# Another order for the first 45 microseconds of a fused attention-plus-MLP block: x on two load queues, the first weights' low parts on GpSimd, x's last 64 columns transposed once

## The chip, the cores and the metric

The kernel runs on one core of one Trainium2 chip. The metric is the device time of one execution in microseconds (us). Before the change the median of three runs is 1194.38 us, from 1193.45 to 1194.89.

## The reference, cut to what matters

The input x has 2048 rows of 576 columns. The output is the sum of x itself, a sliding dilated attention on the layer-normalised x, and a two-layer MLP with ReLU on the same normalised x.

```python
x = A_x                                   # 1 x 2048 x 576
xn = _layernorm(x, axis=-1)
# attention: 32 heads of 18, each row sees 8 rows: itself and 2, 4, ... 14 rows back
qkv = xn @ wqkv                           # 576 x 1728
attn = softmax(q . k[pos - 2*w] * 18**-0.5)   # w = 0..7, rows before 0 masked
a = (sum over w of attn * v[pos - 2*w]) @ wo  # 576 x 576
# MLP
b = relu(xn @ w1) @ w2                    # 576 x 4608, 4608 x 576
return x + a + b
```

## The kernel before, in words

The rows are cut into two phases of 1024 rows, and each phase into eight tiles of 128 rows, named x0 to x7 here. For every tile, `stats` computes mean and variance on VectorE (DVE) and the inverse root on GpSimd (POOL), `norm` applies them on VectorE or, with `act=True`, on ScalarE (ACT), and `make_xt` transposes the result on TensorE (PE) into PSUM and from there writes a high part (ScalarE, rounded to the fast matmul format) and a low part (VectorE, the difference). All matrices are held as such a pair. A product is three sums of terms: high by high, low by high and high by low; the list `TERMS` gives fourteen matmuls for 576 columns, of which the first four use the high part of x and of the weight, the next four the low part of x, the ninth the mixed block of the last 64 columns, and the last five the low part of the weight.

The 576 columns are four blocks of 128 and a rest of 64 (`DR`). In the rest block, high and low part of x share one 128-row tile (`mix`): rows 0 to 63 high, 64 to 127 low. Before the change the 64 columns are first written twice side by side (line 261 for x, line 411 for the attention's output), so that one transpose of 128 columns puts them on both halves of the partitions.

The MLP is a row of slots. Slot n belongs to a phase, a chunk of three hidden blocks of 128, a pair of tiles (`tb`) and one hidden block. `h_mm(n)` multiplies w1 by the pair's transposed x (fourteen matmuls of 256 columns) and evicts the ReLU as a high part on ScalarE (line 447) and a low part on VectorE (line 448). `o_mm(n)` multiplies that by w2 (twelve matmuls of 288 columns) into the PSUM tiles `po`; after the third block of a chunk the sums are added to x on VectorE (line 471). The loop at the end of `tile_body` issues h_mm two slots ahead of o_mm. h0 to h2 read the transposed x0 and x1, h3 to h5 read x2 and x3, h6 to h8 read x4 and x5, h9 to h11 read x6 and x7.

Weights come through a ring of four staging tiles `st` (loads on SP's queue), and `two` splits each into high (line 146, ScalarE) and low (line 143, VectorE). The step at which a split is issued is set by the plan; for the first chunk the six steps stand in `HEADW` (three for w1, three for w2). The next load of the ring is issued when a split has read its staging tile.

The order in the opening is written by hand. Before the loop the loads, the statistics and the norms of x0 to x2, the splits of the first two w1 blocks (`held` puts their low parts behind the low parts of x) and the transposes of x0 and x1 are issued. The list `HEAD` places the remaining `stats`, `norm` and `xt` calls at a step; 0 puts the call behind h_mm of that step, 1 behind o_mm; the last field says whether `norm` runs on ScalarE, or whether `xt` uses the big PSUM tiles `po`. Every engine works its instructions off in the order of issue. Attention work starts later and is spread over VectorE by estimated times (`run_bg`).

## Time and profile before

| | |
|---|---|
| median of three runs | 1194.38 us (1193.45 to 1194.89) |
| profiled execution | 1194.74 us, of which the span is 1193.0 us |
| TensorE (PE) busy | 1183.8 us, 99% of the span |
| VectorE (DVE) busy | 812.5 us, 68% |
| ScalarE (ACT) busy | 310.5 us, 26% |
| GpSimd (POOL) busy | 40.1 us, 3% |
| mean granted TensorE clock | 0.998 |

The profile gives per engine the time in which an instruction ran. A view of waits names who waited for whom. A timeline gives start and duration in us, engine, source line, operation, the tile written and the tiles read, shape and count, and in brackets the idle time before and who ended it. The chain of waits follows the work back from the last instruction. PE's busy time is a modelled one, since matmuls are pipelined; the distance from start to start is what counts.

### The profile page before, as it was taken

To read this page: it belongs to the slowest core of one execution; us is meant where nothing else is said; L and a number is where in the kernel's file an instruction comes from. 1 tells how busy PE (TensorE), PEld (TensorE's weight loads), DVE (VectorE), ACT (ScalarE), POOL (GpSimd) and SP (SyncE) were. 2 spreads that over 40 slices of the span, in tenths; PEclk is the share of its full clock that TensorE was granted. 3 is DMA by queue.
4 is the path that set the end of the run, shared out by engine and by line. 5 is a ranking of instruction groups with operands and counts; after the bars stand their busy time and mean duration, and the time that the engine had idled before them with its cause. 6 is when DMAs were issued, how large, how long until landed. Compare 5 with 4: busy or idle time off the path is not lost.

```text
span 1193.0 us, 21739 instructions
## 1 busy us (share of the span) xinstructions
PE 1183.8 (99%) x9016; PEld 1172.8 (98%) x9016; DVE 812.5 (68%) x1269; ACT 310.5 (26%) x790; POOL 40.1 (3%) x63
## 2 busy tenths in 40 slices
PE   8999999999999999999999999999999999999998
PEld 7999999999999999999999999999999999999998
DVE  7516875888687578875573278858767875886732
ACT  5422222131222222322233123122221322222210
POOL 2000000010000000000120000000100000000000
PEclk9999999999999999999999999999999999999999
DMA  5312122130321311402242113031302312212002
GB/s 172 84 32 82 42 76 55 38 107 1 98 58 44 86 33 43 114 11 73 91 130 74 46 54 90 22 85 29 86 21 79 83 38 79 63 42 73 21 1 80
DMA packets 84883, 75.67 MB, mean 63 GB/s; under 512 B 6592, under 2 KB 68288, under 8 KB 84784
## 3 DMA queue, kind: packets, MB, share of 16 engines
q1 hardware_dynamic: 82256, 66.08, 19.7%
q10 hardware_dynamic: 2528, 8.20, 2.4%
q8 instruction: 71, 1.16, 0.4%
q14 instruction: 28, 0.23, 0.1%
HBM read 61.34 MB, written 4.72 MB: 55 GB/s over the span
## 4 chain that ended last, share of the span: by engine, by line
PE 98%; DVE 1%; SPq 0%; ACT 0%; DMA 0%; issue 0%; DVEq 0%; ACTq 0%
PE ph L112 39%; PE po L112 38%; PE pm L112 20%; PE pm L273 1%; PE pm L274 0%; DMA st<-in_w 0%; SPq L235 0%; DVE pr L380 0%; DVE pr L373 0%; SPq L157 0%; SPq L162 0%; SPq L161 0%; PE po L273 0%; ACT xn L257 0%; ACT xn L256 0%
## 5 line engine op out<-in xcount | busy, mean ns | idle before, releaser
L112 PE MATMUL ph<-xT,w1t 128*128 128x256 f32 x4032 | 514.2, 279 | 1.3 <-ACT xT L276 0.6
L112 PEld LDWEIGHTS ph<-xT,w1t 128*128 128x128 f32 x4032 | 491.6, 188 | 2.0 <-ACT xT L276 0.8
L112 PE MATMUL po<-w2t,hhi 128*128 128x288 f32 x2304 | 400.5, 296 | 0.4 <-DVE w2t L143 0.3
L112 PEld LDWEIGHTS po<-w2t,hhi 128*128 128x128 f32 x2304 | 337.0, 188 | 2.0 <-DVE w2t L143 0.5
L447 ACT ACTIVATE hhi<-ph 128x256 fp32r<-128x256 f32 x288 | 110.2, 382 | 531.8 <-PE ph L112 512.5
L112 PE MATMUL po<-w2t,hlo 128*128 128x288 f32 x1152 | 244.7, 293 | 0.0
L448 DVE SCALAR_TENSOR_TENSOR hlo<-ph,hhi 128x256 fp32r<-128x256 f32 x288 | 121.7, 423 | 169.1 <-ACT hhi L447 167.8
L471 DVE TENSOR_TENSOR x<-po,x 128x576 f32<-128x576 f32 x192 | 143.9, 757 | 69.8 <-PE po L112 66.3
L112 PE MATMUL pm<-wq,xT 128*128 128x432 f32 x896 | 185.5, 358 | 0.0
L112 PEld LDWEIGHTS po<-w2t,hlo 128*128 128x128 f32 x1152 | 183.7, 188 | 0.0
L112 PEld LDWEIGHTS pm<-wq,xT 128*128 128x128 f32 x896 | 163.8, 188 | 5.6
L343 DVE TENSOR_TENSOR pr<-qo,k 128x1152 f32<-128x1152 f32 x64 | 85.9, 1349 | 0.0
L373 DVE TENSOR_TENSOR pr<-lg,v 128x1152 f32<-128x1152 f32 x64 | 85.0, 1352 | 0.3
L346 DVE TENSOR_REDUCE lg<-pr 128x64 f32<-128x1152 f32 x64 | 85.0, 1343 | 0.0
L143 DVE TENSOR_TENSOR w2t<-st,w2t 128x576 fp32r<-128x576 f32 x72 | 54.3, 755 | 45.0 <-ACT w2t L146 44.7
L380 DVE TENSOR_TENSOR pr<-pr 128x288 f32<-128x288 f32 (+1 forms) x128 | 70.5, 602 | 0.1
L143 DVE TENSOR_TENSOR w1t<-st,w1t 128x640 fp32r<-128x640 f32 x72 | 59.0, 820 | 15.0 <-ACT w1t L146 14.8
L146 ACT ACTIVATE w2t<-st 128x576 fp32r<-128x576 f32 x72 | 49.1, 684 | 45.0 <-PE po L112 31.0
L146 ACT ACTIVATE w1t<-st 128x640 fp32r<-128x640 f32 x72 | 53.0, 737 | 13.2 <-DMA st<-in_w 13.2
L312 ACT ACTIVATE k<-pm 128x144 f32<-128x144 f32 x64 | 18.7, 292 | 142.8 <-PE pm L112 142.6
L112 PE MATMUL pm<-wq,oT 128*128 128x288 f32 x352 | 51.7, 299 | 0.0
L112 PEld LDWEIGHTS pm<-wq,oT 128*128 128x128 f32 x352 | 47.9, 188 | 1.7
(63 smaller groups left out, 398.0 us busy)
## 6 DMA issues: line engine op xcount, KB each, us to landing
st<-in_w SPq DMA_DIRECT2D x72, 288.0 KB, 3.0
st<-in_w SPq DMA_DIRECT2D x72, 256.0 KB, 3.0
st<-in_wqkv SPq DMA_DIRECT2D x32, 216.0 KB, 3.0
st<-in_w SPq DMA_DIRECT2D x144, 32.0 KB, 2.7
out<-x SPq DMA_DIRECT2D x16, 288.0 KB, 2.1
x<-in_x SPq DMA_DIRECT2D x15, 288.0 KB, 3.9
k<-k ACTq DMA_DIRECT2D x8, 441.0 KB, 3.9
v<-v ACTq DMA_DIRECT2D x8, 441.0 KB, 4.6
```

The lines of the kernel that those rows point to most:

```text
L112: nc.tensor.matmul(o, l, r, start=start, stop=stop)
L143: nc.vector.tensor_tensor(lo, src, f32(hi), op=ALU.subtract)
L146: nc.scalar.activation(hi, src, AF.Copy)
L273: nc.tensor.transpose(pa[:, k, :], src[:, k * P : (k + 1) * P], ident)
L312: nc.scalar.activation(k[:, W - 1 + i, :], pq[:, 1, :], AF.Copy)
L343: nc.vector.tensor_tensor(pr[i], q, window(k, i), op=ALU.mult)
L346: nc.vector.tensor_reduce(lg[:, i], pr.pop(i).rearrange(heads, d=Dh), axis=AX.X, op=ALU.add)
L373: nc.vector.tensor_tensor(pr[i].rearrange(heads, d=Dh), e, window(v, i).rearrange(heads, d=Dh), op=ALU.mult)
L380: nc.vector.tensor_tensor(o, z[:, 0:n], z[:, n : 2 * n], op=ALU.add)
L447: nc.scalar.activation(hi, pt, AF.Relu)
L448: nc.vector.scalar_tensor_tensor(lo, pt, 0.0, f32(hi), op0=ALU.max, op1=ALU.subtract)
L471: nc.vector.tensor_tensor(acc, PO[k][:, :, 0:D2], acc, op=ALU.add)
```

## The change

- The loads of x1, x2 and x3 are issued on ScalarE's queue; x0 (in two halves) and x4 to x7 stay on SP's. All four staging tiles are loaded before x4. The `Exp` that loads ScalarE's table now follows ScalarE's three loads.
- While `early` holds (the six splits of the first chunk) the low part of a weight is made on GpSimd, not VectorE. `HEADW` moves the first w2 split from step 0 to step -1.
- The 64 last columns are transposed once, into 64 partitions; high and low part are both made from these, the low part written to partitions 64 to 127. The doubling copies on ScalarE (two lines, 32 instructions) are gone.
- `norm` on VectorE subtracts the mean itself, so GpSimd's negation is left only in front of `norm` on ScalarE.
- For x0 and x1 the evictions are interleaved: both high parts, both low parts, both last blocks' high, both last blocks' low.
- `HEAD` is another list. The transposes of x2 and x3 now both stand behind h2 (before: behind h0 and behind h2), those of x4 and x5 behind o2 and behind h5 (before: behind o1 and o2), those of x6 and x7 behind h7 and o5 (before: behind o4 and o5). x2, x3 and x5 are normalised on VectorE, x4, x6 and x7 on ScalarE (before: x5 on VectorE, x2, x3, x4, x6 and x7 on ScalarE).

```diff
@@ -28,24 +28,25 @@
 EPS = 1e-5
 
 UNIT0, UNIT_STEP, WO_AT = 7, 27, 8
-HEADW = (-5, -2, -1, 0, 0, 1)
+HEADW = (-5, -2, -1, -1, 0, 1)
 
 HEAD = (
-    (-2, 0, 'stats', 3),
-    (-2, 1, 'xt', 2, True),
-    (-1, 0, 'stats', 4),
-    (-1, 1, 'norm', 3, True),
-    (0, 0, 'xt', 3, False),
-    (0, 0, 'norm', 4, True),
-    (0, 0, 'stats', 6),
-    (0, 1, 'stats', 5),
-    (1, 1, 'norm', 5, False),
-    (1, 1, 'xt', 4, False),
-    (2, 1, 'xt', 5, False),
-    (2, 1, 'norm', 6, True),
-    (2, 1, 'stats', 7),
-    (4, 0, 'norm', 7, True),
-    (4, 1, 'xt', 6, False),
+    (-2, 1, 'stats', 3),
+    (-2, 1, 'norm', 2, False),
+    (-1, 1, 'norm', 3, False),
+    (0, 0, 'xt', 2, False),
+    (0, 0, 'xt', 3, True),
+    (0, 1, 'stats', 4),
+    (1, 0, 'stats', 5),
+    (1, 1, 'norm', 4, True),
+    (2, 0, 'norm', 5, False),
+    (2, 1, 'xt', 4, False),
+    (3, 0, 'xt', 5, False),
+    (3, 0, 'stats', 6),
+    (3, 1, 'stats', 7),
+    (4, 0, 'norm', 6, True),
+    (4, 1, 'norm', 7, True),
+    (5, 0, 'xt', 6, False),
     (5, 1, 'xt', 7, False),
 )
 HALO = ((0, 112), (112, 127))
@@ -96,7 +97,6 @@
     mhalf = consts.tile([P, 1], F32, name="mhalf")
     nc.gpsimd.memset(mhalf, -0.5)
     spare = consts.tile([P, 1], F32, name="spare")
-    nc.scalar.activation(spare, mhalf, AF.Exp)
 
     warm = ps_o.tile([P, 2, 512], F32, name="po")
     for _ in range(WARM):
@@ -136,18 +136,15 @@
             split(st)
             stage_more()
 
-    held = None
+    early = False
 
     def two(hi, lo, src, n):
-        def rest():
+        nc.scalar.activation(hi, src, AF.Copy)
+        if early:
+            nc.gpsimd.tensor_tensor(lo, src, f32(hi), op=ALU.subtract)
+        else:
             nc.vector.tensor_tensor(lo, src, f32(hi), op=ALU.subtract)
             dve(n)
-
-        nc.scalar.activation(hi, src, AF.Copy)
-        if held is None:
-            rest()
-        else:
-            held.append(rest)
 
     W1, W2, WQ, WO = {}, {}, {}, {}
 
@@ -228,11 +225,11 @@
 
     X, XT, XN, MR = {}, {}, {}, {}
 
-    def load_x(ph, i, parts=1):
+    def load_x(ph, i, queue=nc.sync, parts=1):
         X[ph, i] = xp.tile([P, D], F32, name="x")
         for h in range(parts):
             c = slice(h * D // parts, (h + 1) * D // parts)
-            nc.sync.dma_start(X[ph, i][:, c], x_v[ph, i][:, c])
+            queue.dma_start(X[ph, i][:, c], x_v[ph, i][:, c])
 
     def stats(ph, i):
         xt = X[ph, i]
@@ -243,50 +240,63 @@
             nc.vector.bn_stats(st[:, h, :], xt[:, h * D2 : (h + 1) * D2])
         nc.vector.bn_aggr(mv, st)
         nc.vector.tensor_scalar(mv[:, 1:2], mv[:, 1:2], EPS, None, op0=ALU.add)
-        nm = smp.tile([P, 1], F32, name="nm", bufs=4)
-        nc.gpsimd.tensor_scalar(nm, mv[:, 0:1], -1.0, None, op0=ALU.mult)
         nc.gpsimd.tensor_tensor(r, mv[:, 1:2], mhalf, op=ALU.pow)
-        MR[ph, i] = nm, r
+        MR[ph, i] = mv, r
         dve(700)
 
     def norm(ph, i, act=False):
-        nm, r = MR.pop((ph, i))
-        xn = tmp.tile([P, 640], F32, name="xn")
+        mv, r = MR.pop((ph, i))
+        xn = tmp.tile([P, D], F32, name="xn")
         if act:
-            nc.scalar.activation(xn[:, 0:D], X[ph, i], AF.Identity, bias=nm)
-            nc.scalar.activation(xn[:, 0:D], xn[:, 0:D], AF.Copy, scale=r)
+            nm = smp.tile([P, 1], F32, name="nm", bufs=2)
+            nc.gpsimd.tensor_scalar(nm, mv[:, 0:1], -1.0, None, op0=ALU.mult)
+            nc.scalar.activation(xn, X[ph, i], AF.Identity, bias=nm)
+            nc.scalar.activation(xn, xn, AF.Copy, scale=r)
         else:
-            nc.vector.tensor_scalar(xn[:, 0:D], X[ph, i], nm, r, op0=ALU.add, op1=ALU.mult)
+            nc.vector.tensor_scalar(xn, X[ph, i], mv[:, 0:1], r, op0=ALU.subtract, op1=ALU.mult)
             dve(600)
-        nc.scalar.activation(xn[:, D:640], xn[:, KT * P : D], AF.Copy)
         XN[ph, i] = xn
 
-    def transpose_split(src, last, hi, mix, lo, free=False):
+    def transpose_split(src, hi, mix, lo, free=False, parts=False):
 
         if free:
-            pa, pb = (ps_o.tile([P, 2, 512], F32, name="po")[:, 0, :] for _ in range(2))
-            pa, pb = pa.rearrange("p (k c) -> p k c", k=KT), pb[:, 0:P]
+            po = ps_o.tile([P, 2, 512], F32, name="po")
+            pa, pb = po[:, 0, :].rearrange("p (k c) -> p k c", k=KT), po[0:DR, 1, 0:P]
         else:
             pa = ps_m.tile([P, KT, P], F32, name="pm")
-            pb = ps_m.tile([P, P], F32, name="pm")
+            pb = ps_m.tile([P, P], F32, name="pm")[0:DR]
         for k in range(KT):
             nc.tensor.transpose(pa[:, k, :], src[:, k * P : (k + 1) * P], ident)
-        nc.tensor.transpose(pb, last, ident)
+        nc.tensor.transpose(pb, src[:, KT * P : D], ident)
         t["pe"] += 5 * 0.06
-        nc.scalar.activation(hi, pa, AF.Copy)
-        nc.vector.tensor_tensor(lo, pa, f32(hi), op=ALU.subtract)
-        nc.scalar.activation(mix, pb, AF.Copy)
-        nc.vector.tensor_tensor(mix[DR:P], pb[DR:P], f32(mix[DR:P]), op=ALU.subtract)
-        dve(512)
-        dve(128)
-
-    def make_xt(ph, i, free=False):
+
+        def high():
+            nc.scalar.activation(hi, pa, AF.Copy)
+
+        def low():
+            nc.vector.tensor_tensor(lo, pa, f32(hi), op=ALU.subtract)
+            dve(512)
+
+        def last_high():
+            nc.scalar.activation(mix[0:DR], pb, AF.Copy)
+
+        def last_low():
+            nc.vector.tensor_tensor(mix[DR:P], pb, f32(mix[0:DR]), op=ALU.subtract)
+            dve(128)
+
+        steps = high, low, last_high, last_low
+        if not parts:
+            for f in steps:
+                f()
+        return steps
+
+    def make_xt(ph, i, free=False, parts=False):
         tb, h = divmod(i, 2)
         if h == 0:
             XT[ph, tb] = xtp.tile([P, 9, TBN], F32R, name="xT")
         d = XT[ph, tb][:, :, h * P : (h + 1) * P]
         xn = XN.pop((ph, i))
-        transpose_split(xn[:, 0:512], xn[:, 512:640], d[:, 0:4, :], d[:, 4, :], d[:, 5:9, :], free)
+        return transpose_split(xn, d[:, 0:4, :], d[:, 4, :], d[:, 5:9, :], free, parts)
 
 
     TERMS = [(k, k) for k in range(KT)] + [(5 + k, k) for k in range(KT)] + [(4, 4)] + [(k, 5 + k) for k in range(5)]
@@ -407,10 +417,8 @@
     def wo_a(ph, i):
         assert (ph, i) in ready, (ph, i, len(bg))
         o = QO[ph][:, i, :]
-        od = tmp.tile([P, 2, DR], F32, name="od")
-        nc.scalar.activation(od, o[:, None, KT * P : D].to_broadcast([P, 2, DR]), AF.Copy)
         d = tmp.tile([P, 9, P], F32R, name="oT", bufs=1)
-        transpose_split(o[:, 0:512], od.rearrange("p a b -> p (a b)"), d[:, 0:4, :], d[:, 4, :], d[:, 5:9, :])
+        transpose_split(o, d[:, 0:4, :], d[:, 4, :], d[:, 5:9, :])
         OT[ph, i] = d
 
     def wo_b(ph, i):
@@ -520,32 +528,34 @@
             f(step, *a)
     tasks = deque(sorted(tasks, key=lambda z: z[0]))
 
-    load_x(0, 0, 2)
-    load_x(0, 1)
-    for i in range(1, AHEAD + 1):
-        stage_more(i)
-        load_x(0, 1 + i)
-    for i in range(AHEAD + 2, NI):
+    load_x(0, 0, nc.sync, 2)
+    for i in (1, 2, 3):
+        load_x(0, i, nc.scalar)
+    nc.scalar.activation(spare, mhalf, AF.Exp)
+    stage_more(AHEAD + 1)
+    for i in range(4, NI):
         load_x(0, i)
+    early = True
     stats(0, 0)
     stats(0, 1)
-    held = []
-    run_splits(-5)
     norm(0, 0)
     norm(0, 1)
+    run_splits(-5)
+    first = make_xt(0, 0, parts=True)
+    second = make_xt(0, 1, True, parts=True)
+    for k in range(2):
+        first[k]()
+        second[k]()
+    for k in range(2, 4):
+        first[k]()
+        second[k]()
     stats(0, 2)
-    make_xt(0, 0)
-    make_xt(0, 1, True)
-    for f in held:
-        f()
-    held = None
-    run_splits(-LAG)
-    norm(0, 2, True)
     for z, k, op, *a in HEAD:
         (late if k else at)(z, {"stats": stats, "norm": norm, "xt": make_xt}[op], 0, *a)
     M = (3.0, 1.5, 3.0)
     for n in range(-LAG, len(slots)):
         run_splits(n)
+        early = n < 1
         m = n + LAG
         if m < len(slots):
             h_mm(m)
```

## The prediction

> **What bounds the kernel now.** First the page: span, busy times, the chain that ended last.
>
> ```profile
> span 1193.0 us, 21739 instructions
> ...
> PE 1183.8 (99%) x9016; PEld 1172.8 (98%) x9016; DVE 812.5 (68%) x1269; ACT 310.5 (26%) x790; POOL 40.1 (3%) x63
> ...
> PE 98%; DVE 1%; SPq 0%; ACT 0%; DMA 0%; issue 0%; DVEq 0%; ACTq 0%
> ```
>
> TensorE is the bound: 98% of the chain is its work. A change that touches no matmul of the main loop can only move what TensorE loses, and the diff moves work in the opening. So next the busy time by stretches, and TensorE's waits.
>
> ```profile
> 1.00:2.00 1.00, 0.65 (x3) 0.65 (x4) 0.00 (x0) 1.00 (x1) 0.34 (x2) 1.00 0.18 22
> 2.00:3.00 1.00, 1.00 (x7) 1.00 (x6) 0.05 (x1) 0.21 (x2) 0.00 (x0) 1.00 1.00 295
> ...
> 11.00:12.00 1.00, 0.99 (x5) 0.99 (x5) 0.97 (x2) 0.91 (x2) 0.00 (x0) 0.54 0.96 325
> ...
> 20.00:40.00 20.00, 20.00 (x164) 20.00 (x165) 16.40 (x37) 12.47 (x29) 5.31 (x9) 1.00 0.33 85
> ```
> ```profile
> PE pm L273 <- DVE xn L259: 1.3, 1, 1.3
> PE pm L274 <- ACT xn L261: 0.7, 1, 0.7
> PE ph L112 <- ACT xT L276: 0.6, 1, 0.6
> ```
>
> Columns of the first: stretch, length, busy time (count) of PE, PEld, DVE, ACT, POOL, granted clock, DMA share, GB/s. From 20 us on TensorE has no gap; before, it waits for the normalised and transposed x. The timeline gives the opening, step by step (start, duration).
>
> ```profile
> 2.95 0.88 DVE L243 BATCH_NORM_STATS2 bst<-x 128x6 f32<-128x288 f32 x2 [2.95 <-DMA x<-in_x]
> ...
> 4.42 0.57 POOL L248 TENSOR_TENSOR rstd<-mv,mhalf 128x1 f32<-128x1 f32 x1
> ...
> 5.13 0.82 DVE L243 BATCH_NORM_STATS2 bst<-x 128x6 f32<-128x288 f32 x2 [0.86 <-DMA x<-in_x]
> ...
> 6.23 0.15 DVE L245 TENSOR_SCALAR mv<-mv 128x1 f32<-128x1 f32 x1
> ...
> 6.47 0.84 POOL L248 TENSOR_TENSOR rstd<-mv,mhalf 128x1 f32<-128x1 f32 x1
> ...
> 7.34 0.58 DVE L259 TENSOR_SCALAR xn<-x,nm,rstd 128x576 f32<-128x576 f32 x1 [0.47 <-POOL rstd L248]
> ...
> 7.37 0.74 ACT L146 ACTIVATE w1t<-st 128x640 fp32r<-128x640 f32 x1 [5.14 <-DMA st<-in_w]
> ...
> 9.11 0.60 ACT L276 ACTIVATE xT<-po 128x512 fp32r<-128x512 f32 x1
> ...
> 9.76 0.74 PE L112 MATMUL ph<-xT,w1t 128*128 128x256 f32 x4 [0.58 <-ACT xT L276]
> ...
> 10.26 0.69 DVE L277 TENSOR_TENSOR xT<-po,xT 128x512 fp32r<-128x512 f32 x1
> ...
> 10.98 0.29 DVE L279 TENSOR_TENSOR xT<-po,xT 64x128 fp32r<-64x128 f32 x1
> ...
> 11.31 1.56 DVE L143 TENSOR_TENSOR w1t<-st,w1t 128x640 fp32r<-128x640 f32 x2
> ...
> 21.35 1.78 PE L112 MATMUL ph<-xT,w1t 128*128 128x256 f32 x14
> ...
> 42.73 1.78 PE L112 MATMUL ph<-xT,w1t 128*128 128x256 f32 x14
> ```
>
> The last two rows are my milestones: h3 starts at 21.35, h9 at 42.73. After h9 the order of instructions on each engine is the old one again, and TensorE is full, so what h9 gains or loses stays to the end. In steady state a slot costs, by the chain of waits (start, length):
>
> ```profile
> 23.13 1.59 PE po L112 x12
> ...
> 24.72 0.44 PE pm L273 x4
> 25.15 0.11 PE pm L274
> 25.26 1.61 PE ph L112 x14
> ```
>
> h is 1.61, o 1.59, a tile's five transposes 0.55. Between the milestones lie six h, six o and four tiles: 9.66 + 9.54 + 2.20 = 21.40, and 42.73 - 21.35 = 21.38: no wait at all. The change can't gain there, only lose.
>
> **The change up to h3.** A hand-over between engines is 0.05 (high part ends 9.71, matmul starts 9.76). *Loads.*
>
> ```profile
> x<-in_x SPq DMA_DIRECT2D x15, 288.0 KB, 3.9
> ```
>
> Bytes start at about 1.9 (share 0.18 in the second us) and run at 295 GB/s with the DMA engines at share 1.00: the transfers are the limit already, so the second queue changes who comes first. x0 and x1 now share: 576 KB take 2.0 us, so both land near 4.1 (now x0's second half by 3.4, x1 at 5.13). The Trainium skill, "DMA: Bandwidth & Descriptors", section "Issuing engines are not separate DMA queues", says that queues of several engines run on the same 16 DMA engines and save only the time of issue; by that alone this edit is worth about nothing, and the share of 1.00 agrees.
>
> ScalarE's three issues and the table load behind them cost nothing: it idles until w1 lands (5.14 us of idle before 7.37), and w1's first block, 320 KB behind at most 1152 KB of x, lands by 7.0 at the same rate. The ring's next loads now wait for GpSimd's reads: the second w2 block for the first subtraction (near 8.7) and its turn behind x7. It is needed on ScalarE behind h1, near 15, about when it lands; later, it would hold up h2's ReLU, which stands behind it.
>
> VectorE: a tile's statistics take 1.25 (5.13 to 6.38). x0's second half 0.42 and the rest 0.43 end at 4.95, x1's at 6.25; now 6.38. VectorE's own work has taken the place of the load. Root 0.57 to 0.84, norm 0.58: x1 is normalised at 7.7 (7.92 now). *Single transposes:* the wait of 0.7 for the doubling copy goes; x1's transposes end near 8.25, its high part near 8.9, h0 starts near 8.95 instead of 9.76. The low parts (0.69, 0.69, 0.29, 0.29 and gaps) run from 8.15 to 10.3. Behind them now stand the statistics of x2: 11.6, where before they ended at 9.30.
>
> *GpSimd.* From there its own order decides: root of x2, low part of w1's second block, root of x3, low part of the first w2, low part of w1's third block. The trace has no GpSimd subtraction; the nearest rows are
>
> ```profile
> L349 POOL TENSOR_SCALAR_AFFINE_SELECT lg<-lg 1x512 f32<-1x512 f32 x8 | 9.4, 1172 | 843.7 <-DVE lg L346 843.7
> ...
> L304 POOL MEMSET k<- 1x1008 f32 x8 | 7.4, 930 | 0.0
> ```
>
> 2.29 ns an element where it reads and computes, 0.92 where it only writes: 640 elements cost 0.6 to 1.47, and up to 2.2 if they stretch beside VectorE as the root did (0.57 alone, 0.84 beside the norm at 6.47). I take 1.45 (576 elements: 1.30), because it reads too. Against 0.78 on VectorE (11.31, two in 1.56). The Trainium skill, "GPSIMD Engine Reference", section "Elementwise — side-by-side cycle accounting", gives 4497 ns for 2048 elements, about twice VectorE's time; an estimate from it is 1.4 us, which would leave the sum as it is. No run here shows it yet.
>
> Sum: 0.57 + 1.45 + 0.57 + 1.30 + 1.45 = 5.34, hand-overs 0.2: 11.6 becomes 17.15. All of h1 and the first nine matmuls of h2 fit in between; h2's last five need that low part, and h2 ends at 17.75. Then x2 and x3 are transposed, 1.1, to 18.85. o0's second half takes the PSUM tile that x3's transposes used, so it waits for x3's last low part: x2's high part at 18.9, then 0.69 + 0.29 + 0.69 + 0.29 and gaps, 21.0. Half an o: 0.80. h3 starts at 21.8 against 21.35. The same adding puts the kernel of before at 21.9, 0.55 late, as it counts every hand-over in full; taking off about half of that leaves **+0.2**. Ends: below 0.9 a subtraction, x's own path binds and h3 comes at 20.0 to 20.4, -1.3; at 2.2 it is +2.4. The slow clock (0.54 in the twelfth us) covers matmuls that wait for GpSimd anyway.
>
> **From h3 to h9.** VectorE no longer makes six low parts, but x4 to x7 are normalised and transposed later, each step behind the last. Prices:
>
> ```profile
> 9.21 0.22 POOL L247 TENSOR_SCALAR nm<-mv 128x1 f32<-128x1 f32 x1 [1.90 <-DVE mv L244]
> ...
> 27.05 0.57 ACT L146 ACTIVATE wq<-st 128x432 fp32r<-128x432 f32 x1
> ...
> 27.51 0.39 ACT L447 ACTIVATE hhi<-ph 128x256 fp32r<-128x256 f32 x1
> ...
> 28.08 0.61 DVE L143 TENSOR_TENSOR wq<-st,wq 128x432 fp32r<-128x432 f32 x1
> ...
> 28.72 0.42 DVE L448 SCALAR_TENSOR_TENSOR hlo<-ph,hhi 128x256 fp32r<-128x256 f32 x1
> ...
> 29.07 1.41 DVE L471 TENSOR_TENSOR x<-po,x 128x576 f32<-128x576 f32 x2
> ...
> 29.59 0.78 ACT L256 ACTIVATE xn<-x,nm 128x576 f32<-128x576 f32 x1
> ...
> 30.46 0.78 ACT L257 ACTIVATE xn<-xn,rstd 128x576 f32<-128x576 f32 x1
> ```
>
> *h6 waits for x5.* From h3's end: ReLU high 0.39, low 0.42, x5's statistics 1.25, root 0.57, GpSimd's negation for x4 (queued behind that root) 0.22, x4's two norm passes 1.65, wq high 0.57 (behind them on ScalarE) and low 0.61, h4's low 0.42, x5's norm 0.58, the two additions to x 1.41, x4's low parts 0.98, wq low 0.61, h5's low 0.42, x5's low 0.69: 10.79, with 17 hand-overs of 0.04 11.45. TensorE needs until there o1, h4, o2, x4, h5, x5, o3 and four of h6: 9.55. Wait: 1.9; ScalarE's and VectorE's starts overlap a little, I take **1.6**.
>
> *x6 is late.* From there: x5's last low 0.29, statistics of x6 and of x7 2.50, root of x7 0.57 (ahead of x6's negation in GpSimd's order), 0.22, two passes 1.65: 5.23, with hand-overs 5.45. TensorE has ten matmuls of h6, o4, h7: 4.35. Wait **1.1**.
>
> *o6 waits for the addition into x2.* From x6's norm: x7's passes 1.65, wq high and h7's high 0.96, x6's high 0.60, low 0.98, addition 0.71: 4.90. TensorE: x6, o5, x7, h8, 4.30. Wait **0.6**.
>
> Together 3.3; without any hand-over 2.4, with all 4.0.
>
> **The rest.** 32 transposes now load 64 columns instead of 128 and stream 128. If the load sets their 0.11, half of it goes; if the stream does, nothing. Some six lie in waits: 26 x 0 to 0.055, 0 to -1.4; the trace can't tell, I take the middle, **-0.7**. The 32 copies on ScalarE and 13 negations on GpSimd in front of VectorE's norms are on engines at 26% and 3%: nothing after h9.
>
> Sum: +0.2 + 3.3 - 0.7 = +2.8. The profiled execution took 1194.74 (span 1193.0 and 1.74 around it), so 1197.5; against the median 1194.38, 0.36 lower, **1197.2 us**.
>
> **The rivals.** *GpSimd and the loads are worse (0.20).* x's packets on ScalarE's queue are twice as long as those of x0's halves; if the queues take turns by packet, x0 lands at 5.0 instead of 4.1, and 0.8 goes on top; a subtraction of 1.8 adds another 1.0: +4.6, 1199.0. For it: the root that stretched. *GpSimd is quick (0.12).* At 0.9 or less, h3 gains 1.3, the later waits stay: -1.3 + 3.3 - 0.7 = +1.3, 1195.7. For it: the memset row. *The later waits aren't there, so it is not slower (0.15).* Place: h6. If the steps from h3's end to x5's low part run in 9.55 instead of 11.45, x6 isn't late either: +0.2 - 0.7 = -0.5, 1193.9, and with a quick GpSimd -2.0 to -2.7. For it: VectorE loses six subtractions of 0.78; against it: not one of them lay in that chain.
>
> **How the numbers follow.** About 0.2%, 2.4 us, can be told from no change: 1192.0 to 1196.8. The forecast (0.53) spreads from 1195.0 to 1199.5: 0.36 slower, 0.17 same. The worse case is slower (0.20). Quick GpSimd: 0.10 same, 0.02 faster. No later waits: 0.07 same, 0.08 faster. Sum: faster 0.10, same 0.34, slower 0.56. Range: the two unknown prices and the later waits at their ends give -0.3 to +6.4; towards the third rival it reaches down to 1193.4, and 1200.4 leaves out the far corner.
>
> **What would show it.** Right: GpSimd subtractions near 1.45; h3 near 21.6; TensorE waiting 1 to 2 us for x5's low part inside h6, about 1 for x6's norm; h9 near 46; then no gap. Wrong: h9 at or before 42.7, or subtractions under 0.9, or transposes with 64 columns that still take 0.11.

## The result, and the profile after

| | before | changed |
|---|---|---|
| median of 6 runs, us | 1194.41 (1193.45 to 1195.21) | 1203.16 (1201.84 to 1203.59) |
| profiled execution, span | 1194.74, 1193.0 | 1203.10, 1201.3 |
| h3 starts, h9 starts | 21.35, 42.73 | 25.64, 50.78 |
| h3 to h9 | 21.38 | 25.14 |
| h9 to the end of the span | 1150.3 | 1150.5 |

The ratio is 1.0071, 95% interval 1.0058 to 1.0084: slower by 8.75 us, where 2.8 were forecast. The span grew by 8.3: 4.29 of it before h3, 3.76 between h3 and h9, nothing behind h9. The page of the changed kernel (busy times, chain):

```profile
span 1201.3 us, 21655 instructions
PE 1185.5 (99%) x9016; PEld 1174.5 (98%) x9016; DVE 807.4 (67%) x1265; ACT 302.0 (25%) x754; POOL 44.9 (4%) x56
PE 94%; DVE 2%; DMA 2%; ACT 1%; issue 0%; SPq 0%; POOL 0%; DVEq 0%; POOLq 0%; ACTq 0%
```

TensorE is as busy as before; the chain now runs through other engines for 6% instead of 2%. TensorE's waits (total, times, longest) name them:

```profile
PE ph L112 <- POOL w1t L144: 2.7, 1, 2.7
PE pm L269 <- DVE xT L277: 2.6, 2, 1.5
PE pm L269 <- DVE xn L256: 1.8, 1, 1.8
PE po L112 <- DVE xT L284: 1.7, 1, 1.7
```

The timeline of the changed kernel's opening, in the order of time (x0's two halves, x1's norm and transposes, h0, then GpSimd's chain):

```profile
4.38 0.46 DVE L240 BATCH_NORM_STATS2 bst<-x 128x6 f32<-128x288 f32 x1 [4.38 <-DMA x<-in_x]
5.23 0.46 DVE L240 BATCH_NORM_STATS2 bst<-x 128x6 f32<-128x288 f32 x1 [0.40 <-DMA x<-in_x]
8.22 0.58 DVE L256 TENSOR_SCALAR xn<-x,mv,rstd 128x576 f32<-128x576 f32 x1 [0.45 <-POOL rstd L243]
8.86 1.11 PE L269 MATMUL po<-ident,xn 128*128 128x128 f32 x4 [0.27 <-DVE xn L256]
10.87 6.70 PE L112 MATMUL ph<-xT,w1t 128*128 128x256 f32 x37 [0.69 <-ACT xT L274]
13.29 0.15 DVE L242 TENSOR_SCALAR mv<-mv 128x1 f32<-128x1 f32 x1
14.04 1.55 POOL L144 TENSOR_TENSOR w1t<-st,w1t 128x640 fp32r<-128x640 f32 x1
16.34 0.83 POOL L243 TENSOR_TENSOR rstd<-mv,mhalf 128x1 f32<-128x1 f32 x1 [0.74 <-DVE mv L242]
17.14 1.40 POOL L144 TENSOR_TENSOR w2t<-st,w2t 128x576 fp32r<-128x576 f32 x1
17.30 1.56 DVE L256 TENSOR_SCALAR xn<-x,mv,rstd 128x576 f32<-128x576 f32 x1
18.50 1.75 POOL L144 TENSOR_TENSOR w1t<-st,w1t 128x640 fp32r<-128x640 f32 x1
20.30 0.86 PE L112 MATMUL ph<-xT,w1t 128*128 128x256 f32 x5 [2.74 <-POOL w1t L144]
21.98 0.27 PE L270 MATMUL po<-ident,xn 128*64 128x128 f32 x1
24.03 0.27 ACT L281 ACTIVATE xT<-po 64x128 fp32r<-64x128 f32 x1 [1.14 <-DVE xT L277]
24.76 0.78 PE L112 MATMUL po<-w2t,hhi 128*128 128x288 f32 x4 [1.71 <-DVE xT L284]
25.64 1.78 PE L112 MATMUL ph<-xT,w1t 128*128 128x256 f32 x14
```

Every step of the forecast's chain is there, and the lag behind it grows from one end of it to the other. x1's transposes take 1.11 instead of 0.60; the granted clock was 0.80 in their first us and 0.50 behind that. The windows (length, then PE, PEld, DVE, ACT, POOL, clock, DMA share, GB/s):

```profile
3.00:4.00 1.00, 1.00 (x7) 1.00 (x6) 0.00 (x0) 0.63 (x2) 0.00 (x0) 1.00 1.04 391
9.00:15.00 6.00, 5.31 (x24) 4.86 (x25) 3.46 (x9) 2.63 (x7) 2.85 (x3) 0.50 0.88 285
25.64:50.78 25.14, 22.04 (x178) 21.36 (x177) 15.71 (x39) 12.43 (x26) 6.20 (x10) 1.00 0.21 57
```

Between the milestones TensorE is idle for 3.1 of 25.14. The timeline there (x5's root, the negation for x4 behind it, x4's norm; x5's and x7's transposes; h9):

```profile
29.60 0.56 POOL L243 TENSOR_TENSOR rstd<-mv,mhalf 128x1 f32<-128x1 f32 x1 [1.61 <-DVE mv L242]
30.13 0.23 POOL L252 TENSOR_SCALAR nm<-mv 128x1 f32<-128x1 f32 x1
30.39 0.78 ACT L253 ACTIVATE xn<-x,nm 128x576 f32<-128x576 f32 x1 [2.56 <-POOL nm L252]
35.88 0.66 PE L269 MATMUL pm<-ident,xn 128*128 128x128 f32 x4 [1.48 <-DVE xT L277]
43.47 0.66 PE L269 MATMUL pm<-ident,xn 128*128 128x128 f32 x4 [0.47 <-ACT xn L254]
46.98 0.66 PE L269 MATMUL pm<-ident,xn 128*128 128x128 f32 x4 [1.15 <-DVE xT L277]
50.78 1.78 PE L112 MATMUL ph<-xT,w1t 128*128 128x256 f32 x14
```

ScalarE stood idle 2.56 until the negation for x4 came, 4.75 after h3's start.

### The profile page after: what moved, and what is told of

It is laid out like the page before. It is cut to its first block, busy times and chain, and to the rows that moved or that the text cites. A ratio compares the mean times of both kernels' runs of the same rounds, so it can differ in the third digit from the quotient of the medians.

```text
span 1201.3 us, 21655 instructions
## 1 busy us (share of the span) xinstructions
PE 1185.5 (99%) x9016; PEld 1174.5 (98%) x9016; DVE 807.4 (67%) x1265; ACT 302.0 (25%) x754; POOL 44.9 (4%) x56
## 4 chain that ended last, share of the span: by engine, by line
PE 94%; DVE 2%; DMA 2%; ACT 1%; issue 0%; SPq 0%; POOL 0%; DVEq 0%; POOLq 0%; ACTq 0%
PE ph L112 37%; PE po L112 37%; PE pm L112 20%; DMA st<-in_w 2%; PE pm L269 1%; DVE x L479 0%; DVE xT L277 0%; PE pm L270 0%; SPq L232 0%; DVE pr L353 0%; ACT xn L253 0%; DVE bst L240 0%; DVE w1t L146 0%; POOL w1t L144 0%; ACT xn L254 0%
## 5 line engine op out<-in xcount | busy, mean ns | idle before, releaser
L146 DVE TENSOR_TENSOR w1t<-st,w1t 128x640 fp32r<-128x640 f32 x69 | 56.4, 818 | 13.1 <-ACT w1t L142 12.9
```

The costliest lines, as they stand in the source:

```text
L146: nc.vector.tensor_tensor(lo, src, f32(hi), op=ALU.subtract)
```

## The experiments

"a" kernels are the changed one with something taken back, "b" kernels the one before with a part of the change. Beside them the kernel before took 1194.6 to 1195.1. h3 and h3 to h9 are from one profiled execution each, in which h3 moves with the granted clock; the medians decide. In the code cuts `...` stands for lines left out.

| kernel | median us | ratio to before [95%] | h3 | h3 to h9 |
|---|---|---|---|---|
| a_loads | 1200.89 | 1.0057 [1.0043, 1.0070] | 23.14 | 25.18 |
| a_dvelow | 1201.04 | 1.0050 [1.0037, 1.0062] | 23.44 | 25.11 |
| a_twopo | 1202.29 | 1.0061 [1.0049, 1.0074] | 24.25 | 25.17 |
| a_head | 1202.10 | 1.0063 [1.0050, 1.0075] | 27.97 | 22.09 |
| a_stats2 | 1203.85 | 1.0069 [1.0057, 1.0082] | 24.48 | 25.13 |
| a_warm | 1202.79 | 1.0066 [1.0053, 1.0079] | 25.20 | 25.13 |
| a_nm | 1199.39 | 1.0038 [1.0024, 1.0052] | 26.36 | 21.84 |
| a_nm_x2 | 1198.27 | 1.0029 [1.0018, 1.0039] | 23.16 | 21.83 |
| a_nm_both | 1195.90 | 1.0008 [0.9999, 1.0017] | 21.70 | 21.83 |
| b_loads | 1195.86 | 1.0008 [0.9998, 1.0017] | 22.29 | 21.37 |
| b_pool | 1195.03 | 1.0004 [0.9994, 1.0013] | 21.76 | 21.37 |
| b_single | 1194.04 | 0.9995 [0.9986, 1.0004] | 20.32 | 21.46 |
| b_three | 1196.14 | 1.0009 [1.0001, 1.0018] | 22.12 | 21.46 |
| b_head | 1200.98 | 1.0048 [1.0035, 1.0061] | 24.88 | 23.29 |
| b_head_single | 1199.81 | 1.0042 [1.0029, 1.0056] | 23.18 | 21.89 |
| b_single_one | 1193.43 | 0.9991 [0.9982, 0.9999] | 19.91 | 21.45 |
| best_a | 1193.23 | 0.9988 [0.9979, 0.9997] | 19.21 | 21.43 |
| best_b | 1193.33 | 0.9988 [0.9979, 0.9997] | 20.20 | 21.43 |

**a_nm: the negation moved back.** This settles the loss after h3.

```
     def stats(ph, i):
...
+        nm = smp.tile([P, 1], F32, name="nm", bufs=4)
+        if ph == 0 and i in (4, 6, 7):
+            nc.gpsimd.tensor_scalar(nm, mv[:, 0:1], -1.0, None, op0=ALU.mult)
         nc.gpsimd.tensor_tensor(r, mv[:, 1:2], mhalf, op=ALU.pow)
-        MR[ph, i] = mv, r
+        MR[ph, i] = mv, nm, r
...
     def norm(ph, i, act=False):
...
-            nm = smp.tile([P, 1], F32, name="nm", bufs=2)
-            nc.gpsimd.tensor_scalar(nm, mv[:, 0:1], -1.0, None, op0=ALU.mult)
```

> The changed kernel with the negation of the mean for x4, x6 and x7 made on GpSimd right after that tile's own statistics, as before, instead of at its norm, where it stands behind the next tile's root; all else changed (1203.2, h3 to h9 25.14). Theory: ScalarE's norm of x4 starts 2 after h3's start instead of 4.75, its norm of x6 some 2 earlier, so the waits of x5's, x6's and x7's transposes (1.5, 0.5, 1.2) shrink to below 0.5 together: h3 to h9 near 22, 1200.1. Rival 'the places of the norms and transposes make the waits, whoever negates': h3 to h9 24.5 or more, 1203.

It gave 3.77, and h3 to h9 fell from 25.14 to 21.84. Its timeline after h3 at 26.36 (negation for x4, root, ScalarE's norm of x4):

```profile
26.52 0.23 POOL L245 TENSOR_SCALAR nm<-mv 128x1 f32<-128x1 f32 x1 [5.19 <-DVE mv L241]
26.77 0.57 POOL L246 TENSOR_TENSOR rstd<-mv,mhalf 128x1 f32<-128x1 f32 x1
28.46 0.77 ACT L254 ACTIVATE xn<-x,nm 128x576 f32<-128x576 f32 x1
```

The norm of x4 starts 2.1 after h3 instead of 4.75. A 0.23 us instruction on an engine that is 4% busy had held ScalarE, which held the wq block's high part behind that norm, VectorE's low parts behind it, and so the PSUM tile that x5's transposes wait for. The theory holds; the places of the norms and transposes leave 0.46 (21.84 against 21.38). By the medians the gain is as large (3.77), although the profiled execution, at a clock of 0.995, was the slowest of the five.

**a_loads: x's loads as before.**

```
-    for i in (1, 2, 3):
-        load_x(0, i, nc.scalar)
...
+    load_x(0, 1)
+    for i in range(1, AHEAD + 1):
+        stage_more(i)
+        load_x(0, 1 + i)
     stage_more(AHEAD + 1)
...
```

The `Exp` goes back ahead of the loads, too.

> The changed kernel with x's loads put back on SP's queue in the old interleaved order; all else changed. The changed kernel starts h3 at 25.64 and h9 at 50.78 and takes 1203.2. Theory (the loss up to h3 is shared: loads about 1.1, the rest GpSimd's order, the clock and a shared PSUM tile): x0's two halves are used near 3.0 and 3.4 again, not at 4.38 and 5.23, x1's statistics end 0.9 earlier, h0 starts near 10.0 instead of 10.87 and h3 near 24.6; 1202.1. Rival 'mainly the loads': h3 near 22, 1199.5. Rival 'the loads are hidden behind GpSimd's chain': h3 stays within 0.3 of 25.64, 1203.2. h3 to h9 stays near 25.1 in all three.

x0's halves (timeline) and the windows of that kernel:

```profile
2.93 0.46 DVE L240 BATCH_NORM_STATS2 bst<-x 128x6 f32<-128x288 f32 x1 [2.93 <-DMA x<-in_x]
3.96 0.46 DVE L240 BATCH_NORM_STATS2 bst<-x 128x6 f32<-128x288 f32 x1 [0.56 <-DMA x<-in_x]
...
9.23 3.34 PE L112 MATMUL ph<-xT,w1t 128*128 128x256 f32 x23 [0.69 <-ACT xT L274]
```
```profile
2.00:3.00 1.00, 1.00 (x7) 1.00 (x6) 0.07 (x1) 0.21 (x2) 0.00 (x0) 1.00 1.12 293
3.00:4.00 1.00, 1.00 (x7) 1.00 (x6) 0.44 (x2) 0.00 (x0) 0.00 (x0) 1.00 0.71 220
```

2.27, twice the theory's 1.1, and h0 1.64 earlier: x0 comes 1.3 to 1.45 earlier, and this execution kept the full clock (0.999), which the changed kernel's profile did not. With the clock at 1.000 the changed kernel had a span of 1200.0 and this one 1199.1 and 1199.2, so about 0.9 is the loads themselves, by one such execution of the changed kernel. What of the rest is clock is not separated here.

**a_dvelow: no low part on GpSimd.**

```
-    early = True
...
-        early = n < 1
```

> The changed kernel with every low part on VectorE, none on GpSimd; all else changed. Theory: h2's wait of 2.74 for the third w1 block's low part goes, the norm of x3 takes 0.58 again instead of 1.56, but VectorE has some 0.78 a block more in its order: h3 near 23.3, so 1201. Rival 'mainly GpSimd': h3 at 21.5 to 22, 1199.3. Rival 'GpSimd takes nothing, VectorE would be just as late': h3 at 25 to 26, 1203.

1201.04 and 23.44, as the theory had it, at the same lowered clock as the changed kernel (0.997). Its timeline has the norms of x2 and x3 at their old length:

```profile
16.09 0.57 DVE L256 TENSOR_SCALAR xn<-x,mv,rstd 128x576 f32<-128x576 f32 x1
18.32 0.57 DVE L256 TENSOR_SCALAR xn<-x,mv,rstd 128x576 f32<-128x576 f32 x1
```

**a_nm_both: negation, loads and low parts taken back together.** The diff is that of the three above.

> The changed kernel with the negation moved back (1199.39), x's loads on SP's queue in the old order and all low parts on VectorE; left of the change are the new places and order and the single transposes. Alone, in the changed kernel, the loads taken back gave 2.27 and the low parts 2.12. Theory (they are in series, the gains add): h3 near 22, 1195.0 to 1196. Rival 'loads and GpSimd lie side by side, so only one of the two gains counts': 1197.2. Rival 'the new order on VectorE binds, as in the kernel before with the new places, which took 1199.8': 1199.

1195.90, as the theory had it. Taken back together, loads and GpSimd's low parts give 3.49 behind a_nm; one by one they gave 2.27 and 2.12, so the two lie mostly in series and overlap by 0.9. Since a_nm mostly ran at a clock of 0.997 and this kernel at 0.999 or 1.000, a part of the 3.49 can be clock; the one execution of a_nm at 1.000 took 1198.92. TensorE's largest wait left is o0's for x3's last low part:

```profile
PE po L112 <- DVE xT L285: 1.7, 1, 1.7
```

**a_warm: 33 warm-up transposes instead of 24.** `-WARM = 24`, `+WARM = 33`.

> The changed kernel with 33 instead of 24 warm-up transposes, so that TensorE has no gap of 1.8 between them and x0's transposes (6.04 to 7.82); all else changed. Theory (the gap is what takes the clock to half for one or two stretches in most executions): granted clock 0.999 or 1.000 in nearly all runs, 1201.8, the time that the one undisturbed execution of the changed kernel took. Rival 'the clock falls at its own times': clock 0.995 to 0.997 in most runs, 1203 or more.

The mean clock stayed at 0.998 or above in all five runs, where the changed kernel had 0.995 to 0.997 in five of six. But only 0.37 was gained. The timeline (x3's root, the end of h2, x2's transposes) and one window of that kernel show why:

```profile
15.04 0.77 POOL L243 TENSOR_TENSOR rstd<-mv,mhalf 128x1 f32<-128x1 f32 x1
18.98 1.09 PE L112 MATMUL ph<-xT,w1t 128*128 128x256 f32 x5 [1.96 <-POOL w1t L144]
19.86 1.06 PE L269 MATMUL pm<-ident,xn 128*128 128x128 f32 x4
```
```profile
20.00:21.00 1.00, 1.00 (x7) 0.96 (x6) 0.42 (x1) 0.43 (x2) 0.30 (x1) 0.50 0.53 102
```

With the gap filled, h0 runs at the full clock, x3's root has no idle time before it (0.74 in the changed kernel), and the end of h2 comes 1.32 earlier. But then the clock is halved from about 19.4 to 22.8, behind two waits of TensorE of 1.44 and 1.96, x2's and x3's transposes take 1.06 each, and h3 comes only 0.44 earlier. So in this execution the half clock was moved, not removed, and a gap alone does not decide it: behind the changed kernel's gap of 2.74 (before 20.30) the clock stayed at 1.00. What the half clock costs is open. The changed kernel's one execution at 1.000 was 1.3 below its median, while the one of a_warm at 1.000 took 1203.02.

**a_twopo: x1's last 64 columns in a PSUM tile of their own.**

```
...
             po = ps_o.tile([P, 2, 512], F32, name="po")
+            qo = po if first_done else ps_o.tile([P, 2, 512], F32, name="po")
-            pa, pb = po[:, 0, :].rearrange("p (k c) -> p k c", k=KT), po[0:DR, 1, 0:P]
+            pa, pb = po[:, 0, :].rearrange("p (k c) -> p k c", k=KT), qo[0:DR, 1, 0:P]
...
+    first_done.append(1)      # behind x1's transposes
```

> The changed kernel where x1's last 64 columns get a PSUM tile of their own (as before) instead of the second half of the tile that holds its first 512; all else changed. Theory: ScalarE's last high part of x1 no longer waits 0.60 for VectorE's low part, VectorE's last low part and x2's statistics come 0.3 to 0.6 earlier; h3 the same amount earlier; 1202.7. Rival 'VectorE was busy anyway': h3 within 0.15 of 25.64, 1203.2.

0.87 less, but its profiled execution had the full clock and h0 0.9 earlier for that reason, so the two causes are not told apart. Inconclusive, and x3's shared tile was left as it is.

**a_stats2: x2's statistics ahead of the first tiles' low parts, as before.**

```
+    stats(0, 2)
     first = make_xt(0, 0, parts=True)
...
-    stats(0, 2)          # behind the low parts
```

> The changed kernel with the statistics of x2 ahead of the first two tiles' low parts on VectorE, as before (the change put them behind); all else changed (1203.2; h3 25.64, h3 to h9 25.14). Theory: x2's statistics end near 10.2 instead of 13.44, so GpSimd's second and third subtraction no longer stand behind a root that waits for them; h0's fifth matmul waits 1.3 longer for x's low parts, h3 comes near 24.2; 1201.7. Rival 'the chain on GpSimd is held up by ScalarE's high parts and by h0 anyway': h3 25.4 or later, 1203 or more.

The rival: 1203.85, no gain. GpSimd's second low part started 2.0 earlier, at 12.04, but x3's root still waited for x3's statistics, and the third low part kept h2 waiting for 3.09.

**a_head: the old places of statistics, norms and transposes.** `HEAD` as before as well:

```
-HEADW = (-5, -2, -1, -1, 0, 1)
+HEADW = (-5, -2, -1, 0, 0, 1)
...
     stats(0, 2)
+    norm(0, 2, True)
```

> The changed kernel with the old places of the statistics, norms and transposes of x2 to x7 and the old step of the first w2 block; loads, GpSimd's low parts and single transposes as changed. Theory: h3 to h9 goes from 25.14 to 21.4 to 22.0 (no wait for x5's and x6's low parts); h3 itself between 24 and 26, so 1199.5 (1198 to 1200.5). Rival 'the later waits come from the late opening or from VectorE's load, not from the places': h3 to h9 stays at 24.5 to 25.5, 1203.

h3 to h9 came to 22.09, as the theory had it, but h3 went to 27.97, so only 1.06 was gained. The old places put x2's transposes between h0 and h1, and with x2's statistics still behind the low parts these come too late:

```profile
15.10 0.66 PE L268 MATMUL po<-ident,xn 128*128 128x128 f32 x4 [2.78 <-ACT xn L253]
23.63 0.66 PE L268 MATMUL pm<-ident,xn 128*128 128x128 f32 x4 [2.00 <-ACT xn L253]
```

Places and order belong together; this kernel takes back half of a pair, and its h3 to h9 is short with x4's negation done before h3 again (26.98 in its timeline), which fits what a_nm showed.

**b_loads, b_pool, b_single, b_three: parts of the change in the kernel before.**

```
# b_loads (the Exp goes behind ScalarE's loads, too)
-    load_x(0, 1)
-    for i in range(1, AHEAD + 1):
-        stage_more(i)
-        load_x(0, 1 + i)
-    for i in range(AHEAD + 2, NI):
+    for i in (1, 2, 3):
+        load_x(0, i, 1, nc.scalar)
...
+    stage_more(AHEAD + 1)
+    for i in range(4, NI):
         load_x(0, i)
# b_pool, in two(); early[0] is True until n reaches 1
+        if early[0]:
+            nc.gpsimd.tensor_tensor(lo, src, f32(hi), op=ALU.subtract)
...
# b_single (in wo_a likewise)
-        nc.scalar.activation(xn[:, D:640], xn[:, KT * P : D], AF.Copy)
...
-        transpose_split(xn[:, 0:512], xn[:, 512:640], d[:, 0:4, :], d[:, 4, :], d[:, 5:9, :], free)
+        transpose_split(xn[:, 0:512], xn[:, 512:D], d[:, 0:4, :], d[:, 4, :], d[:, 5:9, :], free)
```

b_three has the three together.

> The kernel before with x loaded as in the change (x0 on SP's queue, x1 to x3 on ScalarE's, then the weights, then x4 to x7), all else as before (h3 21.35, h9 42.73, 1194.7 in fast runs of this study). Taking the new loads out of the changed kernel gave 2.27, 1.0 of it at equal granted clock. Theory (x0's bytes share the DMA engines, everything behind is about 1 later, and TensorE's first matmuls fall into a longer stretch of half clock): h0 0.9 to 1.1 later, h3 22.3 to 23.5, h3 to h9 21.4: 1195.9 to 1197. Rival 'it only costs because GpSimd's chain hangs behind it': h3 within 0.3 of 21.35, 1194.7.

+1.04 by the medians (its interval still reaches 1), at the low end of the theory. Its clock was 0.997 or 0.998 in ten of eleven runs, so the later data and the longer half clock that the theory names are not told apart.

> The kernel before with the first six low parts on GpSimd, all else as before. Taking GpSimd out of the changed kernel gave 2.1. Theory (an in-order chain of 1.55 a block instead of 0.78, beside the roots and negations): h2 and o0 wait for GpSimd, h3 near 23.3, no later wait, 1196.8. Rival 'VectorE is freed and GpSimd is only slow where the changed order puts roots between': h3 21 to 21.6, 1194.7 or less.

+0.21, nearer the rival, whose h3 was 21 to 21.6 (21.76 came); the interval includes no change. GpSimd's subtractions cost 2.1 in the new order and nothing that can be told from zero in the old one. In the old one x2's root doesn't wait for VectorE's low parts; but a_stats2 took that wait out of the new order and gained nothing, so it is not the reason alone, and the reason stays open.

> The kernel before with x's and o's last 64 columns transposed once and the doubling copies gone, all else as before. In the changed kernel a transpose with a load of 64 columns takes the same 0.11 as one with 128. Theory: nothing in the main loop; in the opening the wait of 0.72 for the doubling copy goes, h0 0.3 to 0.7 earlier, but the low parts on VectorE set h1 and h3: h3 0 to 0.5 earlier, 1194.5. Rival (the forecast's middle): 26 transposes of 0.027 less, 1194.0. Rival (half of each load saved): 1193.3.

1194.04, the time of the first rival, though the interval includes no change; and not for its reason: in the profiled execution h0 comes 0.39 earlier, h3 1.03, h9 0.95, and h9 to the end is 1150.4 (before: 1150.3). A part of the 1.03 is clock: x2's transposes take 0.60 here and took 1.05 before. The records of the 64-column part by form, changed kernel and kernel before (min/median/max, ns):

```profile
L270 PEld LDWEIGHTS pm<-ident,qo x16: 110/111/111, 513.2 to 1154.7; 128*64 128x64 f32 x16
L270 PE MATMUL pm<-ident,qo x16: 272/273/273, 513.3 to 1154.8; 128*64 128x128 f32 x16
```
```profile
L274 PEld LDWEIGHTS pm<-ident,od x16: 138/139/141, 504.7 to 1146.3; 128*128 128x128 f32 x16
L274 PE MATMUL pm<-ident,od x16: 272/272/273, 504.8 to 1146.5; 128*128 128x128 f32 x16
```

The load's record is 28 ns shorter, the matmul's not, and the distance from h9 to the end doesn't move. Where another transpose follows, it starts 0.11 later either way (21.44 to 21.55 in the changed kernel, 19.25 to 19.36 in b_head, which loads 128).

> The kernel before with three of the change's parts together: x on two queues, the first low parts on GpSimd, the last 64 columns transposed once; statistics, norms and transposes in the old places and the old order. Alone the three gave +1.04, +0.21 and -0.78 against 1194.8. Theory (the loss is the new places and order, the other three add up): h3 to h9 21.4, h3 21.5 to 22.3, 1195.3. Rival 'the three hamper each other, as the changed kernel with only its places taken back took 1202.1': h3 over 24, 1198 or more.

1196.14, 0.8 above the theory's sum and far below the rival: without the new places and order, the other three parts cost 1.5 (0.1 to 2.2 by the interval).

**b_head, b_head_single: the new places in the kernel before.** `HEAD` as changed, without and with single transposes.

```
-HEADW = (-5, -2, -1, 0, 0, 1)
+HEADW = (-5, -2, -1, -1, 0, 1)
...
-    norm(0, 2, True)
```

> The kernel before with the new places of statistics, norms and transposes of x2 to x7 (and the first w2 block one step earlier), all else as before. Taking the places back in the changed kernel cut h3 to h9 from 25.14 to 22.09 but put h3 2.3 later. Theory (the places cost 3 to 3.7 after h3: x5's and x7's transposes wait for a PSUM tile, x6's norm is late; in the opening they give something back only where GpSimd is the limit): h3 21 to 22, h3 to h9 24.5 to 25.2, 1198. Rival 'the opening gains what it loses later': h3 near 19, h3 to h9 25, 1195.5. Rival 'without GpSimd's low parts the later waits go': h3 to h9 21.4 to 22, 1195.

1200.98, 3 above the theory: the opening lost, too, and behind h3 less was lost than it had (23.29, not 24.5 or more). The doubling copy of x2 on ScalarE waits for VectorE's norm, and two high parts stand behind it (timeline of ScalarE):

```profile
15.50 0.26 ACT L262 ACTIVATE xn<-xn 128x64 f32<-128x64 f32 x1 [2.20 <-DVE xn L260]
15.66 0.67 ACT L147 ACTIVATE w2t<-st 128x576 fp32r<-128x576 f32 x1
16.27 0.74 ACT L147 ACTIVATE w1t<-st 128x640 fp32r<-128x640 f32 x1
```

> The kernel before with the new places of statistics, norms and transposes, and with the last 64 columns transposed once, so that no doubling copy stands on ScalarE behind VectorE's norm of x2. With the doubling copy the new places took 1201.0, h3 24.88, h3 to h9 23.29, and h2 waited 2.59 for a w1 block's high part that stood behind that copy. Theory: that wait falls below 1, the wait of o0 for x3's low parts (2.37) stays, h3 near 23, h3 to h9 23 to 25: 1198.5. Rival 'the copy was only the last in a queue that is late anyway': h2 still waits over 2, h3 24 to 24.5: 1200.2.

The wait of 2.59 fell to 0.86, o0's to 1.80, h3 came at 23.18, and h3 to h9 fell to 21.89: the theory's mechanism in the opening. The median of 1199.81 is over its 1198.5, though, and the profile is the shortest of five runs (spans 1195.2 to 1199.9). Why this kernel takes 3.9 more than a_nm_both, which has the same places but another order in front of them, stays open: the four longer executions left no trace.

**a_nm_x2: x2's transposes between h1 and h2.**

```
-    (0, 0, 'xt', 2, False),
+    (-1, 1, 'xt', 2, False),
```

> The changed kernel with the negation moved back (1199.39) and x2's transposes one step earlier, between h1 and h2, where TensorE waits for GpSimd anyway, instead of behind h2 together with x3's. Theory: x2's low parts are done before x3's transposes, o0's wait for x3's last low part (1.33 in the kernel without this edit, 1.7 in the changed one) shrinks to about 0.6: h3 1.0 earlier, 1198.4. Rival 'h2's wait for GpSimd only moves and o0 stays as late': 1199.4.

1198.27, as expected, but not by the step that was named: o0 still waits 1.33 for x3's last low part. That the gain is x2's transposes standing inside TensorE's wait for GpSimd is likely and not shown.

**b_single_one, best_a, best_b: a faster version.**

```
# b_single_one: b_single, and in two() as in b_pool, but only for the first block
     run_splits(-5)
+    early[0] = False
# best_a: b_single_one, and
-    load_x(0, 1)
+    load_x(0, 1, 2)
...
-    make_xt(0, 0)
-    make_xt(0, 1, True)
+    pieces = make_xt(0, 0, parts=True), make_xt(0, 1, True, parts=True)
+    for k in range(2):
+        for p in pieces:
+            p[k]()
# best_b: best_a, and
-WARM = 24
+WARM = 30
```

`p[0]` splits a tile's 512 columns, `p[1]` its last 64.

> A try for a faster version: the kernel before with the last 64 columns transposed once (1194.04 alone) and only the very first low part on GpSimd, while VectorE is busy with x's low parts. Theory: that block's low part is done near 9.8 instead of 11.9, h0 doesn't wait for it (0.32), VectorE's next low parts come 0.78 earlier, so h2's and o0's waits (0.65 and 0.51) shrink: h3 19.5 to 19.9, 1193.4. Rival 'GpSimd's negation and root of x2 behind that low part make x2 late': h3 20.3 or later, 1194.0 or more.

> A try for a faster version: the kernel before with the last 64 columns transposed once, the very first low part on GpSimd (1193.43 so far), x1 loaded in two halves, and the 64-column parts of x0 and x1 split after both 512-column parts. Theory: x1's first half is in the statistics 0.4 earlier and the norm of x1 0.4 to 0.7 earlier; VectorE's second low part no longer stands behind a 64-column one (0.3): h3 19.2 to 19.5 instead of 19.91, 1192.9. Rival 'one more issue on SP puts the weights later': h3 19.9 or later, 1193.4 or more.

> The same try with 30 instead of 24 warm-up transposes. Theory: no run below clock 0.999, and the runs no longer spread up to 1196: median 0.3 to 0.5 below that of the try with 24. Rival 'the six transposes delay x0's': 0.5 slower than it.

b_single_one and best_a came out within 0.4 of the theory; best_a starts h3 2.1 earlier than the kernel before and is faster than it by 0.12%, interval 0.03% to 0.21%. Six more warm-up transposes changed nothing (the rival's 0.5 did not come either): best_a and best_b hardly lose the clock (0.999 or above in all 22 runs).

## Why the prediction was right or wrong

**Direction right, size wrong.** The bound held, and behind h9 nothing was gained or lost (1150.3 and 1150.5).

**The step that failed is the term "+0.2 up to h3"; it measured +4.29.** Along its own chain, forecast against the timeline above: x1 normalised 7.7, now 8.80; h0 8.95, now 10.87; x2's statistics 11.6, now 13.44; third low part 17.15, now 20.25; x3's transposes done 18.85, now 22.0; o0's second half 21.0, now 24.76. So 1.84 are lost by the end of x2's statistics, 1.26 on GpSimd, 0.6 between x3's transposes and o0, and the deduction of 0.25 was not earned. a_nm_both takes loads and GpSimd's low parts back, and h3 comes at 21.70. One by one (the first point rests on this window of the kernel before, whose loads are all on SP's queue then):

```profile
14.00:15.00 1.00, 1.00 (x9) 1.00 (x8) 0.92 (x3) 0.53 (x2) 0.00 (x0) 0.75 1.06 413
```

- *Loads.* "Both land near 4.1" had two errors. It took 295 GB/s for the limit because the share was 1.00 there; but the two queues moved 391, and the kernel before itself moved 325 at a share of 0.96 and 413 at 1.06 on SP's queue alone. And it let x0 share with x1 alone, 576 KB. By 5 us the windows of the changed kernel add up to 945 KB (23 + 143 + 391 + 388), and x0's second half was still used only at 5.23: bytes of other tiles came ahead of it. The first rival had said this of x0 (5.0). The Trainium skill, "DMA: Bandwidth & Descriptors", section "Issuing engines are not separate DMA queues", says that issuing from several engines saves only the time of issue; by that the edit is worth about nothing. b_loads has +1.04, with x0's first half used at 4.10 instead of 2.95.
- *Half clock.* The forecast said the slow clock would cover matmuls that wait anyway. It fell on x1's transposes and h0, which do not wait, and h0's low part stands on VectorE ahead of x3's statistics; in a_warm, with h0 at the full clock, x3's root comes without idle time and the third low part 1.32 earlier. What it costs in the end is open (a_warm).
- *GpSimd.* The price of a subtraction was near: 1.54 and 1.55 for 640 elements (1.45 taken), 1.40 to 1.43 for 576 (1.30). But the third one of the chain took 1.75 and x3's root 0.83 (0.57 taken), so the five instructions were busy for 6.08 where the sum had 5.34; and x3's root stood behind h0's low part and x3's statistics, idle for 0.74 before 16.34. The two make the 1.26, less 0.2 of hand-overs that did not come. VectorE's norm of x3 was held while GpSimd subtracted, 1.56 instead of 0.57; here this cost nothing by itself, since VectorE then stood idle for 2.75 until h2's ReLU. The Trainium skill, "SBUF — State Buffer", section "SBUF: two separate sides", says that the port pair which VectorE and GpSimd share is locked for a whole instruction, against a VectorE instruction in a two-port mode or with two inputs from SBUF. The trace agrees in that this norm was held (it ends 0.32 after GpSimd's 17.14 + 1.40); in which mode the norm runs no run shows.
- *The shared PSUM tile.* The diff puts x3's last 64 columns into the tile of its first 512, and ScalarE's last high part then waits 1.14 for VectorE's low part (24.03). The forecast had no such wait. What it costs no run separates: a_twopo gave only x1 a tile of its own.

**"3.3 between h3 and h9" measured 3.76; the sum was near, the places were not.** Forecast: 1.6 in h6, 1.1 at x6, 0.6 at o6. Measured by TensorE's late starts: x5's transposes 1.72, x6's 0.64, x7's 1.40, h6 and o6 near nothing; x4's and x6's low parts hold a PSUM tile that the next tile's transposes need, and these stand ahead of the matmuls for which the forecast had them wait. That the second is too high and the third too low, so that the sum fits, is luck. The beginning of the chain was right: with the negation "queued behind that root" the forecast has x4's norm 3.05 behind h3's end, and it started 3.14 behind it (27.25 to 30.39). What the forecast did not say is that this queue is the whole matter: a_nm shows that the negation's move is 3.3 of the 3.76.

**"-0.7 for single transposes" measured nothing.** It was for the 26 transposes that do not lie in waits, most of them behind h9, and from h9 to the end nothing moved; a transpose with 64 columns still takes 0.11, which the forecast had named as a sign of being wrong. b_single's -0.78, not clear of no change, has the same size by chance: its profile gains in the opening, by the wait for the doubling copy, which the forecast had counted inside the term up to h3, and by the clock there.

**Rivals.** The first (GpSimd and loads worse, 1199.0) was the right direction and still 4 too low. Quick subtractions and the absence of later waits did not come.

One way back from the changed kernel to the one before, by medians: the negation 3.77 (a_nm), loads and GpSimd in the new order 3.49 (a_nm_both), new places and order 1.86 (b_single at 1194.04), single transposes -0.78 (1194.82). The steps add up to 8.3 by their making, since each starts where the last ended; another way would share them out differently, as b_head_single's 1199.81 shows. The first two are clear of noise; of the 1.86 no run says which place or order costs it.

## What to carry to other kernels

An instruction that is moved to its user also moves behind everything its engine has queued in between: price it by what is queued ahead of it, on the least busy engine too. Before splitting loads over queues, ask which transfer is needed first, since here it came later on two queues although more bytes moved in all. A part of a hand-made order can't be taken over or back alone: GpSimd's subtractions cost 0.2 (not clear of nothing) in the old order and 2.1 in the new one.

## What the runs showed of the hardware

VectorE's norm of x3, from SBUF, ended 0.32 after the GpSimd subtraction beside it (17.30 + 1.56 = 18.86 against 18.54; in a_warm's trace two norms ended 0.31 and 0.32 after one). VectorE's low parts, with an input from PSUM, kept their 0.69 beside one, and x3's statistics, from SBUF, their 0.81 (both in the changed kernel's trace). The granted clock of the changed kernel was halved for about 6.8 us from 8.6 us on, behind a gap of TensorE of 1.8 us; with 9 more transposes in the gap it was halved from 19.4 us on instead, and behind a longer gap (2.74) it was not. Two queues together moved 391 GB/s in a us in which x0's first half had not yet come, and delivered it 1.4 us later than one queue did; one queue moved 295 one us earlier and 413 in the fifteenth us of the kernel before.
